# Second-layer products evicted one bank at a time, plain activations first: attention and a two-layer network in one Trainium2 kernel

## Chip, cores and metric

The kernel runs on one core of a Trainium2 chip. The metric is the device time of one execution in microseconds; smaller is better. Before the change the median of three runs is 333.38 us (333.01 to 333.63).

## What is computed

Attention over 8 batches of 8 heads, 576 queries each, with 16 extra "beacon" keys ahead of 576 causal ones and 64 numbers a head. Its output, 4608 tokens of 512 numbers, goes through two dense layers, 512 to 2048 to 512, with a leaky ReLU between:

```
scores = scale * np.matmul(q, k_all.transpose(0, 1, 3, 2))
scores = np.where(causal, -1000000000.0, scores)
a = softmax(scores)
x = (a @ v_all), heads side by side           # 4608 x 512
h = x @ w_in                                  # 4608 x 2048
g = np.maximum(0.01 * h, h)
out = g @ w_out                               # 4608 x 512, float32
```

## The kernel before

Two heads of one batch form a **group**; there are 32, numbered g, four to a batch. 512 tokens form a **chunk**; there are nine, numbered i. Attention of later groups and the two layers of earlier chunks are interleaved on TensorE in one order that the program writes out itself (`tc.manual_schedule`, L731): every engine runs its instructions in the order in which the Python issues them. The steps that matter here:

- **Score block** (`block`, L780): three stretches of 512 score columns for two heads (L314), exponentials on ScalarE (L329 and L333), triangles of the causal mask on GpSimd (L289). The first stretch takes two banks of the pool `ps_one`, the others the pool `ps_sc`.
- **Value step** `v(g, half)` (`value`, L374): 12 or 18 matmuls (L359) into a bank of `ps_one`, then reciprocal and multiplication on VectorE (L388, L389).
- **`x_turn(g)`** (L412): two DMA transposes on SyncE's queue (L417, L425) that put a group's output into `xT`, the first layer's input.
- **First-layer step** `u(i, fc)` (`up`, `moe1`, L431): four matmuls of 512 columns (L442) into a bank of `ps_one`; ScalarE's Prelu (L450) evicts them to `gT`. A chunk has 16. Chunk i can start when its last group's `x_turn` has landed: chunk 2 needs group 11, chunk 3 group 15, and so on.
- **Second-layer step** (`down`, `moe2`, L524): chunk 0 is multiplied plainly (L512). Chunks 1 to 8 use a scheme of Strassen and Winograd: `gT` is cut into four blocks a11, a12, a21, a22 by token half and by feature half, and seven products of sums replace eight. A product has two steps (tiles a and b, 128 tokens each) of eight matmuls of 256 columns (L539).

The left operands (`left`, L483) are plain blocks for products 1 (a11), 2 (a12) and 4 (a22); for 5, 6 and 3 they are the sums s1, s2, s4 in `gsum`, and for 7 the sum s3, which overwrites a21. VectorE makes the sums (`token_sums`, L469; L616), four adds for each half of the features; the second four can start only after the Prelu of the chunk's last first-layer step. They wait in the list `due`, and one is issued before each further step; before step 2 of a chunk the rest is issued at once (`add_all`, L638).

The products are built in the order 1, 6, 2, 7, 5, 4, 3 (`PRODUCTS`, L501). Product 2 is added on top of 1 in bank a, which is therefore open from 1 to 2; 4 on top of 7 in bank c; 3 on top of 5 in bank d. `combine` (L552) evicts: ScalarE copies 1, 2 and 5 (L565, L570, L576), VectorE adds the others (L567, L573, L577, L581, L585), and `store` (L591) writes quarter results to HBM by SyncE's queue. All of this, the first layer, the value steps and the score blocks' first stretches share the four banks of `ps_one`.

Which step comes next is decided by `fill` (L598): first and second layer in turn where both can go. The events of the groups (loads N from HBM by GpSimd, L171; key and query transposes T by SyncE, L179; blocks, value steps, `x_turn`) have due times, and the loop at L817 puts as many steps between them as their share of the work at hand. When a batch's last group is finished, three second-layer steps that were kept back (`KEPT`, L668) go first. Before a value step, the loop fills up to four steps since the last block, if no second-layer step is to be had (L826).

Of the kernel before, what the change touches and what calls it, by code (L numbers as in the profile page):

```python
# [8 lines left out]
FP32 = mybir.dt.float32  # L9
# [6 lines left out]
def kernel(  # L16
# [11 lines left out]
    nc = tc.nc  # L28
# [3 lines left out]
    DM = moe_w_in.shape[0]  # L32
# [6 lines left out]
    NCH = NTOK // 512  # L39
# [42 lines left out]
    opool = ctx.enter_context(tc.tile_pool(name="opool", bufs=2))  # L82
    ps_sc = ctx.enter_context(tc.tile_pool(name="ps_sc", bufs=2, space=bass.MemoryType.PSUM))
    ps_one = ctx.enter_context(tc.tile_pool(name="ps_one", bufs=4, space=bass.MemoryType.PSUM))
# [368 lines left out]
    ADD, SUB = ALU.add, ALU.subtract  # L453

    def weight_sums(part):
        b11, b12 = w_out_sb[:, 0:HF, 0:HD], w_out_sb[:, 0:HF, HD:DM]
        b21, b22 = w_out_sb[:, HF:NF, 0:HD], w_out_sb[:, HF:NF, HD:DM]
        t1, t2, t4 = (w_sum[:, i] for i in range(3))
        tt = nc.vector.tensor_tensor
        if part == 0:  # L460
            tt(out=t1, in0=b12, in1=b11, op=SUB)
            tt(out=t2, in0=b22, in1=t1, op=SUB)
            tt(out=t4, in0=b21, in1=t2, op=SUB)
        else:
            tt(out=b12, in0=b22, in1=b12, op=SUB)
# [17 lines left out]
    def left(i, n, fc, tile):  # L483
        t = slice(tile * 128, (tile + 1) * 128)
        if n == 1:
            return gT[i][:, fc, t]
        if n == 2:
            return gT[i][:, HF + fc, t]
        if n == 7:
            return gT[i][:, fc, HT + tile * 128 : HT + (tile + 1) * 128]  # L490
        if n == 4:
            return gT[i][:, HF + fc, HT + tile * 128 : HT + (tile + 1) * 128]
        return sums[i][{5: 0, 6: 1, 3: 2}[n]][:, fc, t]

    def right(n, fc):
        if n in (5, 6, 4):
            return w_sum[:, (5, 6, 4).index(n), fc]
        fc0, d0 = {1: (0, 0), 2: (HF, 0), 3: (HF, HD), 7: (0, HD)}[n]
        return w_out_sb[:, fc0 + fc, d0 : d0 + HD]

    PRODUCTS = (1, 6, 2, 7, 5, 4, 3)  # L501
    banks, parts = {}, {}

    def ND(i):
        return NF if i == 0 else 2 * len(PRODUCTS)

    def moe2_plain(i, t, quarter):
        if quarter == 0:
            banks["a"] = ps_one.tile([128, 512], FP32, name="acc", tag="one")
        acc = banks["a"]  # L510
        for fc in range(quarter * 4, quarter * 4 + 4):
            nc.tensor.matmul(  # L512
                out=acc,
                lhsT=gT[i][:, fc, t * 128 : (t + 1) * 128],
                rhs=w_out_sb[:, fc],
                start=(fc == 0),
                stop=(fc == NF - 1),
            )
        if quarter == 3:
            osb = opool.tile([128, DM], FP32, name="osb", bufs=3)  # L520
            nc.vector.tensor_copy(out=osb, in_=acc)
            nc.sync.dma_start(out=out[i * 512 + t * 128 : i * 512 + (t + 1) * 128], in_=osb)

    def moe2(i, n2):  # L524
        if i == 0:
            moe2_plain(i, n2 // 4, n2 % 4)
            if n2 == NF - 1:
                weight_sums(1)
            return
        n, tile = PRODUCTS[n2 // 2], n2 % 2  # L530
        bank = {1: "a", 2: "a", 6: "b", 7: "c", 4: "c", 5: "d", 3: "d"}[n]
        opens = n in (1, 6, 7, 5)
        apart = i == NCH - 1 and bank == "d"
        if opens and (tile == 0 or apart):
            banks[bank, tile] = ps_one.tile([128, 512], FP32, name="acc", tag="one")
        acc = banks[bank, tile if apart else 0]
        lo = 0 if apart else tile * HD
        for fc in range(HF):
            nc.tensor.matmul(  # L539
                out=acc[:, lo : lo + HD],  # L540
                lhsT=left(i, n, fc, tile),
                rhs=right(n, fc),
                start=(opens and lo == 0 and fc == 0),
                stop=(fc == HF - 1),
                skip_group_check=True,
            )
        if apart:
            combine(i, n, acc[:, 0:HD], (tile, tile + 1))
        elif tile == 1:
            combine(i, n, acc, (0, 2))  # L550

    def combine(i, n, acc, tiles):  # L552
        lo, hi = tiles[0] * HD, tiles[1] * HD

        def kept(name, bufs=1):
            if lo == 0 or name == "osb":
                parts[name] = opool.tile([128, 512], FP32, name=name, bufs=bufs)
            return parts[name][:, lo:hi]

        def part(name):  # L560
            return parts[name][:, lo:hi]

        tt = nc.vector.tensor_tensor
        if n == 1:
            nc.scalar.copy(out=kept("u2"), in_=acc)  # L565
        elif n == 6:
            tt(out=part("u2"), in0=acc, in1=part("u2"), op=ADD)  # L567
        elif n == 2:
            c = kept("osb", 3)
            nc.scalar.copy(out=c, in_=acc)  # L570
            store(i, 0, 0, tiles, c)
        elif n == 7:
            tt(out=kept("u3"), in0=acc, in1=part("u2"), op=ADD)  # L573
        elif n == 5:
            c = kept("p5")
            nc.scalar.copy(out=c, in_=acc)  # L576
            tt(out=part("u3"), in0=part("u3"), in1=c, op=ADD)  # L577
            store(i, 1, 1, tiles, part("u3"))
        elif n == 4:
            c = kept("osb", 3)  # L580
            tt(out=c, in0=acc, in1=part("u2"), op=ADD)  # L581
            store(i, 1, 0, tiles, c)
        elif n == 3:
            c = kept("osb", 3)
            tt(out=c, in0=acc, in1=part("u2"), op=ADD)  # L585
            store(i, 0, 1, tiles, c)

    def store(i, half, cols, tiles, c):
        t0 = i * 512 + half * HT + tiles[0] * 128
        n = tiles[1] - tiles[0]  # L590
        nc.sync.dma_start(  # L591
            out=out[t0 : t0 + n * 128, cols * HD : (cols + 1) * HD].rearrange("(t p) d -> p t d", p=128),
            in_=c.rearrange("p (t d) -> p t d", t=n),
        )

    done1, done2, at2, ready, turn, first_down, held = [0], [0], [0, 0], [0], [0], [0], [0]

    def fill():  # L598
        i1, fc = divmod(done1[0], NF)
        i2, n2 = at2  # L600
        can1 = i1 < ready[0] and (i1 < 2 or i2 > i1 - 2)
        can2 = i2 < NCH and i2 < i1 and done1[0] >= first_down[0]
        if held[0] and can2:
            held[0] -= 1
            down()
        elif can1 and (turn[0] == 0 or not can2):
            up()
        elif can2:
            down()
        return can1 or can2  # L610
# [8 lines left out]
    def add_all(i):  # L619
        while due and due[0][0] == i:  # L620
            add_due()
# [3 lines left out]
    def up():  # L625
        i1, n = divmod(done1[0], NF)
        assert i1 < ready[0]
        fc = n if i1 == 0 else n // 2 + n % 2 * HF
        moe1(i1, fc)
        add_due()  # L630
        done1[0] += 1
        turn[0] = 1
        if i1 and n % (2 * SLICE) == 2 * SLICE - 1:
            due.extend((i1, op) for op in token_sums(i1, n // 2 + 1 - SLICE, n // 2 + 1))

    def down():
        add_due()
        if at2[1] == 2:  # L638
            add_all(at2[0])
        moe2(*at2)  # L640
        done2[0] += 1
        at2[1] += 1
        if at2[1] == ND(at2[0]):
            at2[:] = at2[0] + 1, 0
        turn[0] = 0
# [19 lines left out]
            )  # L665

    NG = B * NPAIR
    KEPT = 3  # L668

    def has(g):  # L670
        return 0 <= g < NG
# [6 lines left out]
    def finish(g, eng=0):  # L678
        if eng < 2 and g in xs:
            x_transposes(g, (dve, act)[eng])  # L680
        ready[0] = chunks_with(g)
        if g % NPAIR == NPAIR - 1:
            turn[0] = 1
            held[0] = KEPT

    def run(steps):
        for step in steps.split():
# [52 lines left out]
    with order:  # L740
# [46 lines left out]
        def has_down():  # L787
            return at2[0] < done1[0] // NF

        since = 0  # L790
# [26 lines left out]
        for at, _, what, args in events:  # L817
            while w + 2 < len(ends) and at > ends[w + 1]:
                w, d0 = w + 1, done1[0] + done2[0]
            todo = NF * ready[0] + sum(ND(i) for i in range(ready[0])) - KEPT - d0  # L820
            aim = d0 + todo * (at - ends[w]) / (ends[w + 1] - ends[w])
            while done1[0] + done2[0] < aim and fill():
                pass
            if what is block:
                since = done1[0] + done2[0]
            elif what is value and not has_down():  # L826
                while done1[0] + done2[0] < since + 4 and fill():
                    pass
            what(*args)
        while at2[0] < NCH:  # L830
# [31 lines left out]
```

## Time and profile before

| | before |
|---|---|
| median of three runs | 333.38 us |
| profiled execution | 332.48 us |
| its span | 330.8 us |
| TensorE busy | 317.8 us (96%), 3401 matmuls recorded |
| ScalarE busy | 199.8 us (60%) |
| GpSimd busy | 183.2 us (55%), all of it in the first 276 us |
| VectorE busy | 132.5 us (40%) |
| first-layer matmuls L442 | 134.0 us, 615 recorded |
| second-layer matmuls L539 | 47.2 + 32.9 + 15.5 + 15.4 us, 896 recorded |

A time in the profile counts from the start of the span. PE is TensorE's matmul queue, PEld its weight loads, DVE VectorE, ACT ScalarE, POOL GpSimd, SP SyncE. A wait "A <- B" means that A's engine was idle until B ended. Some matmul records are missing, so counts are a little low.

### The profile page before, as it was taken

The numbers are of one execution on the slowest core, as the hardware profiler recorded it, in microseconds if no ns is written. First come the engines' busy times: TensorE is split into PE (matmuls) and PEld (weight loads), VectorE is DVE, ScalarE is ACT, GpSimd is POOL, SyncE is SP. The second block draws the span as 40 slices with busy tenths as digits, with TensorE's granted clock in tenths as the row PEclk, the third lists the DMA queues.
The fourth block names the chain that finished last, engine by engine and source line by source line (L and its number), as shares of the span: only waits on it lengthen the run. The fifth ranks groups of instructions, "written<-read, shape, count | busy, mean of one in ns | idle before, by whom it ended". The sixth has DMA issues, their size and how long they took to land.

```text
span 330.8 us, 8482 instructions
## 1 busy us (share of the span) xinstructions
PE 317.8 (96%) x3401; PEld 213.1 (64%) x3429; DVE 132.5 (40%) x280; ACT 199.8 (60%) x336; POOL 183.2 (55%) x354
## 2 busy tenths in 40 slices
PE   8999999999899999999999999998999999999996
PEld 5574555455586557844778888655875695466685
DVE  3572357126443145414621453334442642333343
ACT  4969861678665784578645865587458514644420
POOL 8895968979987884669546976686221000000000
PEclk9999999999999999999999999999999999999999
DMA  8999999999999999999989999999431113000113
GB/s 134 140 204 178 153 209 121 179 181 131 180 111 169 158 157 142 131 164 102 145 122 154 109 146 113 184 120 155 55 100 37 36 21 127 2 0 34 64 43 117
DMA packets 155929, 39.93 MB, mean 121 GB/s; under 512 B 143041, under 2 KB 153153, under 8 KB 155889
## 3 DMA queue, kind: packets, MB, share of 16 engines
q0 software_dynamic: 99824, 18.54, 83.1%
q1 hardware_dynamic: 55792, 20.77, 38.7%
q8 instruction: 27, 0.44, 0.6%
q14 instruction: 14, 0.11, 0.1%
q10 hardware_dynamic: 272, 0.07, 0.1%
HBM read 37.22 MB, written 9.44 MB: 141 GB/s over the span
## 4 chain that ended last, share of the span: by engine, by line
PE 76%; DMA 8%; ACT 5%; DVE 4%; POOL 4%; issue 2%; SPq 0%; ACTq 0%; POOLq 0%
PE acc L442 34%; PE acc L539 25%; PE av L359 7%; PE sc L314 5%; DMA w_out_sb<-in_moe_w_out_dram 4%; PE acc L512 4%; DMA v_aug<-in_v_dram 3%; DVE gsum L616 2%; ACT aT L333 2%; ACT aT L329 2%; ACT gT L450 1%; DVE x_nat L389 1%; POOL gsum L158 1%; DMA xT<-x_nat 1%; POOL v_aug L214 1%
## 5 line engine op out<-in xcount | busy, mean ns | idle before, releaser
L442 PE MATMUL acc<-xT,w_in_sb 128*128 128x512 bf16 (+1 forms) x615 | 134.0, 357 | 1.9 <-DMA xT<-x_nat 0.5
L450 ACT ACTIVATE gT<-acc 128x512 bf16<-128x512 f32 x144 | 83.0, 620 | 56.9 <-PE acc L442 55.4
L442 PEld LDWEIGHTS <-w_in_sb 128*128 128x128 bf16 x640 | 59.6, 98 | 53.6 <-issue 4.3
L289 POOL TENSOR_SCALAR_AFFINE_SELECT aT<-aT 128x256 bf16<-128x256 bf16 (+2 forms) x160 | 59.8, 403 | 60.9 <-ACT aT L329 38.7
L539 PEld LDWEIGHTS <-gT 128*128 128x128 bf16 x512 | 48.9, 98 | 11.2 <-ACT gT L450 2.3
L333 ACT ACTIVATE aT<-sc 128x1024 bf16<-128x1024 f32 (+3 forms) x64 | 51.7, 890 | 0.0
L539 PE MATMUL acc<-w_out_sb,gT 128*128 128x256 bf16 x384 | 47.2, 273 | 1.4 <-ACT gT L450 1.3
L329 ACT ACTIVATE aT<-sc 128x512 bf16<-128x512 f32 (+3 forms) x64 | 28.9, 520 | 25.3 <-PE sc L314 25.3
L359 PEld LDWEIGHTS <-aT 128*128 128x128 bf16 (+1 forms) x960 | 36.6, 98 | 9.3 <-issue 3.0
L539 PEld LDWEIGHTS <-gsum 128*128 128x128 bf16 x384 | 36.1, 98 | 8.8 <-DVE gsum L616 3.3
L359 PE MATMUL av<-v_aug,aT 128*128 128x65 bf16 (+1 forms) x960 | 39.5, 194 | 1.9 <-ACT aT L329 1.6
L214 POOL DMA_DIRECT2D v_aug<-in_v_dram x40 | 34.3, 866 | 4.3 <-DMA w_in_sb<-in_moe_w_in_dram 4.0
L171 POOL DMA_DIRECT2D q_nat<-in_q_dram x48 | 34.9, 734 | 0.7
L171 POOL DMA_DIRECT2D k_nat<-in_k_dram x48 | 34.8, 732 | 0.7 <-DMA w_out_sb<-in_moe_w_out_dram 0.4
L539 PE MATMUL acc<-w_sum,gsum 128*128 128x256 bf16 x256 | 32.9, 273 | 1.8 <-DVE gsum L616 1.7
L616 DVE TENSOR_TENSOR gsum<-gT 128x1024 bf16<-128x1024 bf16 x16 | 11.2, 697 | 53.9 <-ACT gT L450 53.9
L389 DVE TENSOR_TENSOR x_nat<-av,rec 128x384 bf16<-128x384 f32 (+1 forms) x64 | 31.4, 490 | 2.2
L388 DVE RECIPROCAL rec<-av 128x6 f32<-128x6 f32 (+1 forms) x64 | 11.9, 185 | 50.7 <-PE av L359 50.5
L276 ACT ACTIVATE aT<-sc 128x1024 bf16<-128x1024 f32 (+3 forms) x32 | 26.0, 874 | 3.7 <-PE sc L267 1.9
L314 PE MATMUL sc<-qT,kT 64*128 64x80 bf16 (+22 forms) x384 | 22.4, 250 | 1.2 <-PE acc L442 0.5
L314 PEld LDWEIGHTS <-kT 64*128 64x128 bf16 x384 | 13.3, 94 | 11.9 <-issue 8.9
L573 DVE TENSOR_TENSOR u<-acc,u 128x512 f32<-128x512 f32 x8 | 5.5, 691 | 27.2 <-PE acc L539 27.2
(63 smaller groups left out, 221.5 us busy)
## 6 DMA issues: line engine op xcount, KB each, us to landing
out_dram<-osb SPq DMA_DIRECT2D x27, 256.0 KB, 2.8
q_nat<-in_q_dram POOLq DMA_DIRECT2D x48, 72.0 KB, 4.8
k_nat<-in_k_dram POOLq DMA_DIRECT2D x48, 72.0 KB, 5.2
v_aug<-in_v_dram POOLq DMA_DIRECT2D x24, 128.0 KB, 6.4
w_in_sb<-in_moe_w_in_dram POOLq DMA_DIRECT2D x2, 1024.0 KB, 12.3
w_out_sb<-in_moe_w_out_dram POOLq DMA_DIRECT2D x2, 1024.0 KB, 11.6
out_dram<-u SPq DMA_DIRECT2D x7, 256.0 KB, 2.3
gsum<-in_q_dram POOLq DMA_DIRECT2D x8, 144.0 KB, 6.4
```

Of the source, the lines that this page charges most:

```text
L171: nc.gpsimd.dma_start(out=t[:, :, par], in_=(q, k)[which][b, 2 * hp + par].rearrange("(t p) d -> p t d", p=NR),)
L214: nc.gpsimd.dma_start(out=dst[lo : ROWS[c], c, :, 0:D], in_=v[b, :, OFF[c] : OFF[c] + n].rearrange("h p d -> p h d"),)
L276: nc.scalar.activation(out=aT[:, :, c0 : c0 + w], in_=sc[:, :, 0:w], func=AF.Exp, scale=0.125)
L289: nc.gpsimd.affine_select(out=view, in_=view, compare_op=ALU.is_ge, fill=0.0, base=128 - n if lo == 0 else 0, channel_multiplier=-1, patte ...
L314: nc.tensor.matmul(out=(sc[par] if apart else sc[:, par])[:, at : at + b - a], lhsT=kT[ps_, c * 128 : (c + 1) * 128], rhs=qT[ps_, q0 : q0 ...
L329: nc.scalar.activation(out=probs[g][:, par, lo:hi], in_=sc[par][:, at : at + hi - lo], func=AF.Exp, scale=0.125)
L333: nc.scalar.activation(out=probs[g][:, :, lo:hi], in_=sc[:, :, at : at + hi - lo], func=AF.Exp, scale=0.125)
L359: nc.tensor.matmul(out=avv[:, n, 0 : D + 1], lhsT=aT[0 : ROWS[c], par, a0 : a0 + 128], rhs=va[0 : ROWS[c], c, 2 * hp + par, :], start=(c = ...
L389: nc.vector.tensor_tensor(out=x_nat[:, t0:t1].rearrange("p t e d -> p (t e) d"), in0=avv[:, :, 0:D], in1=rec[:, n0:n1, None].to_broadcast( ...
L442: nc.tensor.matmul(out=acc[:, lo:hi], lhsT=w_in_cols(fc, j), rhs=xT[:, j, x0 : x0 + hi - lo], start=(j == 0), stop=(j == NJ - 1), skip_gro ...
L450: nc.scalar.activation(out=gT[i][:, fc, :], in_=acc, func=AF.Prelu, alpha=0.01)
L539: nc.tensor.matmul(out=acc[:, lo : lo + HD], lhsT=left(i, n, fc, tile), rhs=right(n, fc), start=(opens and lo == 0 and fc == 0), stop=(fc ...
```

## The change

Each product is now evicted as soon as its two steps are done, and opens and closes a bank of its own. The order is 1, 4, 6, 2, 7, 5, 3. ScalarE copies 1, 4 and 5 to SBUF tiles p1, p4, p5; VectorE makes the four results from these and from PSUM with two more adds a chunk, both on SBUF alone (in the last chunk one of the two is made in halves). The output tiles `osb`, three deep, are gone: p1, p4, u3 and p5, one deep, are stored instead, chunk 0's results too. The sums' remainder is issued before step 4. Of a chunk, four second-layer steps are counted out of the share of the work (`KEPT`), and two (`LEAD`) go first at a batch's end. When at most two second-layer steps of the chunk before are left (`LAST`), the first layer goes on and leaves them. Before a value step the loop now fills two steps if second-layer steps are to be had, and then takes these.

```
-    PRODUCTS = (1, 6, 2, 7, 5, 4, 3)
+    PRODUCTS = (1, 4, 6, 2, 7, 5, 3)
...
-            osb = opool.tile([128, DM], FP32, name="osb", bufs=3)
+            osb = opool.tile([128, DM], FP32, name=("p1", "p4", "p5", "u3")[t], bufs=1)
...
-        bank = {1: "a", 2: "a", 6: "b", 7: "c", 4: "c", 5: "d", 3: "d"}[n]
-        opens = n in (1, 6, 7, 5)
-        apart = i == NCH - 1 and bank == "d"
-        if opens and (tile == 0 or apart):
-            banks[bank, tile] = ps_one.tile([128, 512], FP32, name="acc", tag="one")
-        acc = banks[bank, tile if apart else 0]
+        apart = i == NCH - 1 and n2 >= 10
+        if tile == 0 or apart:
+            banks["p"] = ps_one.tile([128, 512], FP32, name="acc", tag="one")
+        acc = banks["p"]
...
-                start=(opens and lo == 0 and fc == 0),
+                start=(lo == 0 and fc == 0),
...
+        if n in (1, 4, 5):
+            nc.scalar.copy(out=part(f"p{n}", True), in_=acc)
+        if n == 6:
+            add(part("u2", True), acc, part("p1"))
         elif n == 2:
+            add(part("p1"), acc, part("p1"))
+            store(i, 0, 0, tiles, part("p1"))
         elif n == 7:
+            add(part("u3", True), acc, part("u2"))
+            add(part("p4"), part("u3"), part("p4"))
+            store(i, 1, 0, tiles, part("p4"))
         elif n == 5:
+            add(part("u3"), part("u3"), part("p5"))
             store(i, 1, 1, tiles, part("u3"))
+            add(part("p5"), part("u2"), part("p5"))
         elif n == 3:
+            add(part("p5"), acc, part("p5"))
+            store(i, 0, 1, tiles, part("p5"))
...
-        elif can1 and (turn[0] == 0 or not can2):
+        elif can1 and not (rest and can2) and (turn[0] == 0 or not can2 or (i1 == i2 + 1 and ND(i2) - n2 <= LAST)):
             up()
...
-        if at2[1] == 2:
+        if at2[1] == 4:
             add_all(at2[0])
...
-    KEPT = 3
+    KEPT, LEAD = 4, 2
...
-            held[0] = KEPT
+            held[0] = LEAD
...
-            elif what is value and not has_down():
-                while done1[0] + done2[0] < since + 4 and fill():
+            elif what is value:
+                while done1[0] + done2[0] < since + (2 if has_down() else 4) and fill(True):
                     pass
```

More of the change, by code (lines that the diff above doesn't have):

```diff
@@ L553, in combine, with part, add @@
         lo, hi = tiles[0] * HD, tiles[1] * HD
-        def kept(name, bufs=1):
-            if lo == 0 or name == "osb":
-                parts[name] = opool.tile([128, 512], FP32, name=name, bufs=bufs)
+        def part(name, new=False):
+            if new and lo == 0:
+                parts[name] = opool.tile([128, 512], FP32, name=name, bufs=1)
             return parts[name][:, lo:hi]
[L560 to L567, printed above, removed]
+        def add(to, x, y):
+            nc.vector.tensor_tensor(out=to, in0=x, in1=y, op=ADD)
+        if n in (1, 4, 5):
+            nc.scalar.copy(out=part(f"p{n}", True), in_=acc)
+        if n == 6:
+            add(part("u2", True), acc, part("p1"))
         elif n == 2:
-            c = kept("osb", 3)
-            nc.scalar.copy(out=c, in_=acc)
-            store(i, 0, 0, tiles, c)
+            add(part("p1"), acc, part("p1"))
+            store(i, 0, 0, tiles, part("p1"))
         elif n == 7:
-            tt(out=kept("u3"), in0=acc, in1=part("u2"), op=ADD)
+            add(part("u3", True), acc, part("u2"))
+            add(part("p4"), part("u3"), part("p4"))
+            store(i, 1, 0, tiles, part("p4"))
         elif n == 5:
-            c = kept("p5")
-            nc.scalar.copy(out=c, in_=acc)
-            tt(out=part("u3"), in0=part("u3"), in1=c, op=ADD)
+            add(part("u3"), part("u3"), part("p5"))
             store(i, 1, 1, tiles, part("u3"))
[L579 to L582, printed above, removed]
+            add(part("p5"), part("u2"), part("p5"))
         elif n == 3:
-            c = kept("osb", 3)
-            tt(out=c, in0=acc, in1=part("u2"), op=ADD)
-            store(i, 0, 1, tiles, c)
+            add(part("p5"), acc, part("p5"))
+            store(i, 0, 1, tiles, part("p5"))
     def store(i, half, cols, tiles, c):
@@ L596, with fill @@
     done1, done2, at2, ready, turn, first_down, held = [0], [0], [0, 0], [0], [0], [0], [0]
-    def fill():
+    LAST = 2
+    def fill(rest=False):
         i1, fc = divmod(done1[0], NF)
```

## The prediction, on record before the change was run

> **What bounds the kernel now.** I read the page's first part, then the waits, the timelines of the engines that the waits name, and last the chain. TensorE first:
>
> ```profile
> PE 317.8 (96%) x3401; PEld 213.1 (64%) x3429; DVE 132.5 (40%) x280; ACT 199.8 (60%) x336; POOL 183.2 (55%) x354
> ```
>
> It is busy 96% of 330.8 us and the change leaves it every matmul, so only its stalls can go. The waits (total, times, longest) say which:
>
> ```profile
> PEld L539 <- DVE gsum L616: 3.3, 6, 0.8
> ...
> PEld L539 <- ACT gT L450: 2.3, 3, 0.9
> ...
> PE acc L539 <- DVE gsum L616: 1.7, 5, 0.6
> PE av L359 <- ACT aT L329: 1.6, 3, 0.8
> ...
> PE acc L539 <- ACT gT L450: 1.3, 2, 0.7
> ...
> PE acc L442 <- DMA xT<-x_nat: 0.5, 1, 0.5
> ```
>
> The weight loads wait beside the matmuls behind them, so I count only the PE rows. On TensorE's timeline (start, length, then idle time and releaser in brackets) one chunk's turn from first to second layer is:
>
> ```profile
> 229.29 0.28 PE L539 MATMUL acc<-w_out_sb,gT 128*128 128x256 bf16 x1 [0.67 <-ACT gT L450]
> ...
> 230.65 0.60 PE L539 MATMUL acc<-w_sum,gsum 128*128 128x256 bf16 x4
> 231.80 0.61 PE L539 MATMUL acc<-w_sum,gsum 128*128 128x256 bf16 x4 [0.55 <-DVE gsum L616]
> ...
> 232.81 1.04 PE L539 MATMUL acc<-w_sum,gsum 128*128 128x256 bf16 x8
> 233.68 0.49 PE L539 MATMUL acc<-w_out_sb,gT 128*128 128x256 bf16 x3
> ```
>
> Product 1 waits for the Prelu of the last but one first-layer step; product 6 waits, halfway, for VectorE's sums. A third kind, in another window, is a value step that wants a PSUM bank while two banks are held by half-built products:
>
> ```profile
> 169.45 0.83 PE L314 MATMUL sc<-qT,kT 64*128 64x176 bf16 x14
> 171.08 0.53 PE L359 MATMUL av<-v_aug,aT 128*128 128x65 bf16 x12 [0.80 <-ACT aT L329]
> ```
>
> A group's record runs some 0.16 us past its last issue slot (the eight matmuls at 232.81 are 1.04 long, yet the next group starts 0.87 later), so a gap of g costs g + 0.16. I use 0.87 for a step of either layer.
>
> The second limit is the feed. The chain shows TensorE waiting for an activation transpose on SyncE's queue:
>
> ```profile
> 101.80 0.56 SPq L417
> ...
> 102.42 3.73 DMA xT<-x_nat
> 106.19 0.59 PE acc L442 x2
> ```
>
> That is the first step u(2,0) of chunk 2, waiting for x_turn(11). On SyncE, in order, that transpose stood behind the key transpose of group 15, and this behind its loads from GpSimd:
>
> ```profile
> 99.25 1.20 SPq L179 DMA_TRANSPOSE kT<-k_nat  x1
> 100.54 1.83 SPq L417 DMA_TRANSPOSE xT<-x_nat  x1
> 102.42 1.22 SPq L425 DMA_TRANSPOSE xT<-x_nat  x1
> ```
>
> GpSimd's timeline shows what set those loads:
>
> ```profile
> 78.49 1.86 POOL L289 TENSOR_SCALAR_AFFINE_SELECT aT<-aT 128x256 bf16<-128x256 bf16 x3 [0.44 <-ACT aT L329]
> 80.60 0.41 POOL L289 TENSOR_SCALAR_AFFINE_SELECT aT<-aT 128x256 bf16<-128x256 bf16 x1 [0.25 <-ACT aT L333]
> ...
> 91.69 1.45 POOL L171 DMA_DIRECT2D k_nat<-in_k_dram  x2
> ```
>
> From 81 to 98 us GpSimd shows no idle time: its loads there do not come earlier because TensorE is faster.
>
> [...] here L567 (from PSUM) and L577 (SBUF alone) both take 692 ns, which I use. [...] at 101.00 VectorE ends a 3.19 us wait for ScalarE's copy of product 5, and only then does the reciprocal behind it run.
>
> **The change, part by part.** The base is the profiled execution: 332.48 us, 1.7 of it outside the span; the runs' median, 333.38, is 0.9 above it.
>
> *Waits removed.* In the new order products 1 and 4 come first, so between the last Prelu and product 6 stand four steps (3.5 us) in place of two, often with two products of the chunk before ahead of them. The sums need two adds of 0.69 after that Prelu: product 6 came at most 0.55 late, so 1.74 more covers it. Product 1's waits (0.63 at 87.13, 0.67 at 229.29) are covered where two old steps or both value steps (0.9) now stand before it. The value waits go because no bank is held across products: each turns over after two steps. Gaps up to 121.5 us: 0.19 (71.06, a first-layer step wanting a bank), 0.63, 0.28 (90.47, the same for a score tile), 0.30; 1.40 and four times 0.16 = 2.04. Later: 0.55, 0.17, 0.53, 0.80, 0.27, 0.67, 0.55, 0.17 = 3.71, eight times 0.16 = 1.28, and 0.31 inside the group at 123.49 (1.35 long, not 1.04): 5.30. Together 7.3.
>
> *What is late next.* u(2,0). The new order has chunk 1's product 3 (two steps) and a score block (0.78) after it, not before: 2 x 0.87 + 0.78 = 2.52 of work moves behind. TensorE, which would have been there at 106.19 - 0.69 = 105.50, arrives at 105.50 - 2.52 - 2.04 = 100.94. The feed hardly moves: the score block before GpSimd's solid stretch comes some 1.2 earlier (a step of 0.87, and the wait at 71.06), but GpSimd was idle only 0.44 then, so x_turn(11) lands at 106.15 - 0.44 = 105.71. TensorE waits 4.8 us: the first 2.04 are lost again, and from there 2.52 - 0.44 = **2.08 more** remains. Before that, group 14's key transpose (in use 1.3 us after landing) is overtaken too; that wait lies inside the same one. The later chunks' first steps stood 5 to 8 us behind their transposes and move 0 to 2.5: no wait. The wait for group 17's keys at 121.48 (0.36 + 0.16 = **0.52**) goes, as TensorE is then later.
>
> *Waits added.* Product 3 is opened, then held over up to nine first-layer steps, so three times a step just after a score block needs the bank of the step just before it: 0.66 us of matmuls against 0.20 (last slot 176.38 to Prelu 176.58) + 0.60 (Prelu) + 0.05: 0.19 each, 0.57. If ScalarE is 0.6 behind, 0.8 each: 2.4; below nothing is excluded, since a wait can't give time. What queues behind is all of TensorE, and through it the next block's exponentials. The block behind u(2,0) comes 2.5 late, so group 18's loads do too; its 3.5 us of cover shrink to under 1: 0 to 1, I take 0.3. Sum **0.87**.
>
> *Work added.* 17 adds of 0.69 or 0.43 on VectorE, 11 us on an engine 40% busy. Those for products 7 and 5 lie ahead of reciprocals; the tightest bank behind them has 1.4 us of matmuls against 0.69 more in the queue: nothing; with that cover gone, 0.69 a chunk. ScalarE keeps three copies a chunk (0.60, now for 1, 4, 5), SyncE four stores, GpSimd all it had. Product 7's store waits for two adds, not one: 0.7 on SyncE, hidden while SyncE is behind its producers. The single buffers p1 to p5 are rewritten 10 us or more after their store: nothing. The tail is as before, 5b's two adds of 0.43 ending before 3b's matmuls: 0 to 0.1.
>
> **Sum**: -5.30 - 0.52 + 2.08 + 0.87 = -2.87. Span 327.9, execution 329.6, on the median's scale 333.38 - 2.87 = **330.5**.
>
> **Rivals.** *The feed gives more.* If x_turn(11) lands 2 us sooner (TensorE's own steps no longer delay group 14's block, and the transposes find a shorter queue), 328.5. For it: those transposes took 3.7 to 7.4 us, so there is room. Against: SyncE waited for the key loads, which GpSimd paces. *The removed waits turn into others*: Prelu late by 0.8 three times (2.4 for 0.57) and group 18 by 1.0 (for 0.3): 330.5 + 2.5 = 333.0, no change. For it: two banks serve the first layer there. Against: ScalarE idles 0.28 before each Prelu of such a stretch, so it isn't behind. *Slower*: x_turn(11) meets a full queue, as x_turn(10) did (issued 92.20, its SyncE row 3.15 long, some 7.3 to landing where x_turn(11) took 3.7), because GpSimd's loads for group 17 now start earlier beside it. Each us there is a us at the end; from a landing at 108.6 the gain is gone, at 109.6 the time is 330.5 + 3.9 = 334.4. Against: the loads move by 1.3 at most.
>
> **Numbers.** Forecast 0.60 (330.5, own spread 329.5 to 331.8), more gain 0.20 (328.5), no change 0.12, slower 0.08. A measurement tells 0.2% (0.7 us) from none: faster 0.79, same 0.13 (a bit of the forecast's upper edge included), slower 0.08. The range runs from 328.5 to 333.2: the upper end takes in the 2.4 for the Prelus, the lower the 2 us of feed.
>
> **Signs.** Right: no PE wait on the sums (gsum, line L610 after the change), none of av on aT; one long PE wait on xT near 101 to 106 us, 4 to 5 us; VectorE some 11 us busier. If that wait is under 2 us, the feed was paced by TensorE and the gain is larger. If first-layer steps wait for Prelus by more than 1 us in all, the held bank is dearer than I say. Wrong altogether: x_turn(11) landing after 108.6.

## The result and the profile after

| | before | after |
|---|---|---|
| median of 20 runs each, in turn on one chip | 332.84 us (331.38 to 338.48) | 333.74 us (332.06 to 337.40) |
| ratio, 95% interval | | 1.0038 (1.0016 to 1.0060) |
| profiled execution, its span | 332.48, 330.8 us | 333.21, 331.5 us |
| mean granted TensorE clock, profiled execution | 0.999 | 0.995 |

The kernel became slower by 0.9 us where 2.87 less was forecast. On the scale of these 20 runs the forecast is 332.84 - 2.87 = 329.97, so 3.8 us are missing. Here and below, medians are of all runs, while ratios, and averages of runs with a like clock, leave out the few executions that fell into a slower state of the chip.

The page's first part, after:

```profile
PE 319.8 (96%) x3429; PEld 213.5 (64%) x3429; DVE 145.9 (44%) x297; ACT 200.1 (60%) x336; POOL 187.5 (57%) x354
```

VectorE is 13.4 us busier (11 were forecast) and GpSimd, which got no new work, 4.3. The waits of TensorE (total, times, longest):

```profile
PE sc L314 <- POOL kT L229: 2.7, 1, 2.7
...
PE av L359 <- DVE x_nat L389: 0.5, 2, 0.3
PE acc L442 <- DMA xT<-x_nat: 0.5, 1, 0.5
...
PE acc L442 <- ACT gT L450: 0.4, 2, 0.2
```

No product waits for the sums any more, none for a Prelu, and no value step for ScalarE's exponentials. In the chunk whose turn was shown before, TensorE's timeline now has no idle time:

```profile
230.19 1.91 PE L537 MATMUL acc<-w_out_sb,gT 128*128 128x256 bf16 x16
...
232.59 1.91 PE L537 MATMUL acc<-w_sum,gT 128*128 128x256 bf16 x16
```

These are products 1 and 4; product 6, at 235.21, follows a score block without idle time too. What was meant to go has gone, then. What came instead stands at the start of chunk 2, on the same timeline:

```profile
96.41 0.52 PE L314 MATMUL sc<-qT,kT 64*128 64x144 bf16 x10
99.59 0.50 PE L314 MATMUL sc<-qT,kT 64*128 64x256 bf16 x6 [2.66 <-POOL kT L229]
100.02 3.57 PE L537 MATMUL acc<-w_out_sb,gT 128*128 128x256 bf16 x16
...
108.32 0.38 PE L442 MATMUL acc<-xT,w_in_sb 128*128 128x512 bf16 x1 [0.53 <-DMA xT<-x_nat]
```

Three losses lie here. A score block waits 2.66 us for group 14's keys; the last of them to arrive is the key transpose, landed at 99.45, not the column copy that the row names: TensorE starts 0.14 after it, the same as in run 7 below (99.49 and 99.63). Then 16 second-layer matmuls take 3.57, not the 1.91 of the chunk above, 1.66 too long. Then u(2,0) waits 0.53 for x_turn(11), which lands at 108.28 by the chain:

```profile
103.66 4.62 DMA xT<-x_nat
```

The windows of this stretch (length, busy time of TensorE, its loads, VectorE, ScalarE and GpSimd, then the granted clock; the last two columns are the DMA's) say what the second loss is:

```profile
90.00:100.00 10.00, 7.34 (x105) 5.77 (x103) 4.32 (x8) 5.04 (x10) 10.00 (x19) 1.00 1.95 129
100.00:110.00 10.00, 9.47 (x96) 6.82 (x94) 4.78 (x9) 3.85 (x7) 5.61 (x12) 0.83 1.50 162
```

The granted clock was 0.83 over 10 us. In narrower windows it was 0.50 from 100.1 to 103.3 us, and 1.00 before 99.9 and after 103.5: 1.7 us lost in some 3.4 at half the clock. GpSimd was busy for the whole ten microseconds before. It was late for two reasons. At 75.62 it was 1.93 behind before already (73.69 there), as this execution as a whole was. And where it could have caught up, its selects (L289) took longer:

```profile
79.98 3.36 POOL L289 TENSOR_SCALAR_AFFINE_SELECT aT<-aT 128x256 bf16<-128x256 bf16 x4
...
88.96 3.57 POOL L289 TENSOR_SCALAR_AFFINE_SELECT aT<-aT 128x256 bf16<-128x256 bf16 x5
```

That is 0.84 and 0.71 each. Before, three took 1.86 and one 0.41 at 78.5 to 81.0, and then five took 2.66, also with some of VectorE's adds beside them:

```profile
86.78 2.66 POOL L289 TENSOR_SCALAR_AFFINE_SELECT aT<-aT 128x256 bf16<-128x256 bf16 x5
```

So group 15's key loads were issued at 94.79, 3.10 later than before. VectorE worked beside the first four on SBUF alone:

```profile
79.97 1.51 DVE L465 TENSOR_TENSOR w_out_sb<-w_out_sb 128x2048 bf16<-128x2048 bf16 x1
81.42 0.88 DVE L610 TENSOR_TENSOR gT<-gT 128x1024 bf16<-128x1024 bf16 x1
```

Both sides took longer side by side: the first four selects 0.84 each here and 0.34 to 0.41 in a kernel where none of VectorE's adds ran beside them, L465 1.51 here and 1.22 in that kernel (experiment 7). What they hold each other up with, the traces don't show.

### The profile page after: what moved, and what is told of

Read it like the earlier page. It is cut to its first block, busy times and chain, and to the rows that moved or that the text cites. A ratio compares the mean times of both kernels' runs of the same rounds, so it can differ in the third digit from the quotient of the medians.

```text
span 331.5 us, 8537 instructions
## 1 busy us (share of the span) xinstructions
PE 319.8 (96%) x3429; PEld 213.5 (64%) x3429; DVE 145.9 (44%) x297; ACT 200.1 (60%) x336; POOL 187.5 (57%) x354
## 3 DMA queue, kind: packets, MB, share of 16 engines
q1 hardware_dynamic: 55792, 20.77, 36.8%
## 4 chain that ended last, share of the span: by engine, by line
PE 67%; DMA 16%; ACT 4%; POOL 4%; DVE 4%; issue 3%; SPq 1%; DVEq 0%; ACTq 0%; POOLq 0%
PE acc L442 28%; PE acc L537 25%; PE av L359 6%; PE sc L314 5%; DMA gsum<-in_q_dram 5%; DMA xT<-x_nat 3%; DMA w_out_sb<-in_moe_w_out_dram 3%; DMA v_aug<-in_v_dram 3%; ACT aT L333 3%; PE acc L512 2%; DMA k_nat<-in_k_dram 2%; POOL aT L289 1%; DVE p L559 1%; DVE u L559 1%; POOL gsum L158 1%
## 5 line engine op out<-in xcount | busy, mean ns | idle before, releaser
L442 PE MATMUL acc<-xT,w_in_sb 128*128 128x512 bf16 (+1 forms) x640 | 136.8, 358 | 1.4 <-DMA xT<-x_nat 0.5
L289 POOL TENSOR_SCALAR_AFFINE_SELECT aT<-aT 128x256 bf16<-128x256 bf16 (+2 forms) x160 | 64.0, 429 | 55.3 <-ACT aT L329 34.1
L537 PE MATMUL acc<-w_out_sb,gT 128*128 128x256 bf16 x384 | 47.9, 279 | 0.0
L562 ACT COPY p<-acc 128x512 f32<-128x512 f32 (+1 forms) x25 | 14.5, 581 | 41.2 <-PE acc L537 37.6
L537 PE MATMUL acc<-w_sum,gsum 128*128 128x256 bf16 x256 | 31.9, 273 | 0.0
```

The costliest lines, as they stand in the source:

```text
L289: nc.gpsimd.affine_select(out=view, in_=view, compare_op=ALU.is_ge, fill=0.0, base=128 - n if lo == 0 else 0, channel_multiplier=-1, patte ...
L442: nc.tensor.matmul(out=acc[:, lo:hi], lhsT=w_in_cols(fc, j), rhs=xT[:, j, x0 : x0 + hi - lo], start=(j == 0), stop=(j == NJ - 1), skip_gro ...
L537: nc.tensor.matmul(out=acc[:, lo : lo + HD], lhsT=left(i, n, fc, tile), rhs=right(n, fc), start=(lo == 0 and fc == 0), stop=(fc == HF - 1) ...
```

## The experiments

**The theory**: the new products gain about what was forecast, and the changed order of steps (KEPT, LEAD, LAST and the fill before value steps) gives it back at one place, where chunk 2's start and group 14's block now come before their feed. **Rivals**: the halved clock alone takes the gain; the held product 3 and the new fill cost a little in every chunk; the new products themselves cost.

| run | kernel | median, us | ratio to before, 95% |
|---|---|---|---|
| 1 | after, TensorE kept busy before group 14's block | 333.81 | 1.0024 (1.0000 to 1.0048) |
| 2 | new products, old order of steps | 328.08 | 0.9872 (0.9841 to 0.9903) |
| 3 | old products, changed order | 336.08 | 1.0111 (1.0073 to 1.0149) |
| 4 | before, with four rests of TensorE | one execution, 351.09 | |
| 5 | after, KEPT 3 and LEAD 3 | 327.28 | 0.9823 (0.9782 to 0.9865) |
| 6 | run 2, plain products not first | 330.01 | 0.9901 (0.9859 to 0.9943) |
| 7 | after, VectorE's adds apart from the selects | 331.47 | 0.9944 (0.9919 to 0.9969) |
| 8 | new products, changed order from chunk 2 on | 328.85 | 0.9847 (0.9803 to 0.9892) |
| 9 | after, KEPT 3 alone | 334.73 | 1.0044 (1.0022 to 1.0066) |
| 10 | after, LEAD 3 alone | 331.60 | 0.9957 (0.9931 to 0.9983) |
| 11 | run 5 up to chunk 2's start, after from there | 329.11 | 0.9886 (0.9829 to 0.9943) |

**1. Is it the clock?** Ten blank matmuls of 512 columns stand ahead of the stretch that first needs group 14.

```
+        for _ in range(warm):
+            nc.tensor.matmul(
+                out=sc[:, 0, 0:512].rearrange("p (r w) -> p r w", w=128),
+                lhsT=blank,
+                rhs=blank[:, None, 0:128].to_broadcast([128, 4, 128]),
...
-                stretch(parts, apart=n == 0)
+                stretch(parts, apart=n == 0, warm=10 if any(g == 14 and lo == 0 for g, lo, _ in parts) else 0)
```

> The changed kernel with ten matmuls of 512 columns on zeros (2.2 us of TensorE work) put where TensorE idled 2.66 us for group 14's keys; nothing else differs, and the results are the same. Theory C (the loss is the clock: after that idle time the matmuls were issued at half pace for 3.4 us): the idle time shrinks to some 0.5 us, the slow pace after it is gone, and the kernel is 1.7 us or more faster than the changed one: ratio to before 0.996 or less. Rival W (the loss is in the added adds and evictions, wherever they lie): the clock makes no difference, ratio about 1.004 as for the changed kernel.

Measured: 333.81 us, no gain, so the ratio of at most 0.996 that one theory gave was missed. The idle time at group 14's block is gone and the matmuls after it have their full pace (16 in 1.92), but TensorE's timeline then reads:

```profile
107.89 0.58 PE L451 MATMUL acc<-xT,w_in_sb 128*128 128x512 bf16 x1 [3.27 <-DMA xT<-x_nat]
108.41 1.46 PE L323 MATMUL sc<-qT,kT 64*128 64x272 bf16 x16
```

(This kernel's lines stand nine further down.) TensorE arrives earlier at u(2,0), waits 3.27 us for x_turn(11), landed at 107.85, and slows down after that (16 score matmuls in 1.46, not 0.83). Although TensorE was ready earlier, u(2,0) began when its transpose landed: the feed sets it, and the clock is a second loss on top. The 22 runs say how large: the six with a mean clock of 1.000 took 331.65 us on average, the thirteen at 0.995 334.15, and before 332.68 at 1.000. So without a slow stretch this kernel gains 1.0 us, not 2.87: the clock is part of the loss, not all of it.

**2 and 3. The products or the order?** Run 2 is the kernel after with the order's rules of before, run 3 the kernel before with the changed rules:

```
-    KEPT, LEAD = 4, 2
+    KEPT, LEAD = 3, 3
...
-        elif can1 and not (rest and can2) and (turn[0] == 0 or not can2 or (i1 == i2 + 1 and ND(i2) - n2 <= LAST)):
+        elif can1 and (turn[0] == 0 or not can2):
...
-            elif what is value:
-                while done1[0] + done2[0] < since + (2 if has_down() else 4) and fill(True):
+            elif what is value and not has_down():
+                while done1[0] + done2[0] < since + 4 and fill():
```

> The changed kernel with the order of steps of before (three steps kept, three to lead, first layer and second in turn, no filling ahead of value steps while second-layer steps are to be had): new products, banks and evictions alone. Theory C: group 14's block keeps its place, so it waits for its keys by 0.7 to 1.5 us[...]; u(2,0) keeps its place too; the waits for sums and banks after 122 us go: some 3 to 4 us faster than before, ratio 0.988 to 0.992. Rival W: the new products bring nothing or a loss, ratio 1.000 to 1.004.

> The kernel before with the changed order of steps alone (four kept, two to lead, LAST, filling ahead of value steps), products and banks as before. Theory C: group 14's block and u(2,0) come early against their feed, and the waits for sums and banks stay: a wait of 1 to 2.5 us on group 14's keys, ratio 1.002 to 1.010. Rival W: as the products are those of before, ratio 0.995 to 1.000.

Measured: 328.08 us for the products alone, 336.08 for the order alone. The products gain 4.8 us against the 332.83 of before, measured in turn with them; the order costs 3.3 without them and 5.7 with them. Run 3 shows the loss at the same place, 4.18 us of waiting for group 14's keys at 100.20 (1 to 2.5 expected), and is a little slower than the range said; a bank is held over there too, and TensorE waits six times more, 0.36 to 0.59 each. In run 2 group 14's block, expected to wait 0.7 to 1.5, doesn't wait; u(2,0) still waits 1.27 us and product 1 three times for a Prelu (0.63, 0.67, 0.67).

**4. What idle time halves the clock?** The kernel before, with four rests of TensorE in chunk 8's first layer: a blank matmul, a Prelu, some selects on GpSimd, then a matmul that needs them.

```
+    RESTS = {0: 2, 5: 4, 10: 5, 15: 7}
...
+        if i1 == NCH - 1 and n in RESTS:
+            rest(RESTS[n])
```

> The kernel before with four rests put into TensorE's work late in the kernel, where nothing is fed any more, at steps 0, 5, 10 and 15 of the last chunk's first layer, some 9 us apart: a matmul on zeros, a Prelu of it, then 2, 4, 5 and 7 triangle selects on GpSimd in a chain, then a matmul that needs them: idle times of some 1.5, 2.3, 2.7 and 3.5 us. Theory C: after the last one or two the next matmuls are issued at half pace for some 3 us, after the first not. Rival W: the pace after all four is the full one, and the slow pace in the changed kernel had another cause.

Measured, on TensorE's timeline (the row that ends each of the first three rests, and work after the first and third):

```profile
292.84 0.23 PE L636 MATMUL av<-blank,aT 128*128 128x128 bf16 x1 [2.23 <-POOL aT L289]
...
295.19 1.91 PE L442 MATMUL acc<-xT,w_in_sb 128*128 128x512 bf16 x4
...
306.34 0.23 PE L636 MATMUL av<-blank,aT 128*128 128x128 bf16 x1 [2.80 <-POOL aT L289]
...
318.27 0.29 PE L636 MATMUL av<-blank,aT 128*128 128x128 bf16 x1 [2.91 <-POOL aT L289]
318.35 1.91 PE L442 MATMUL acc<-xT,w_in_sb 128*128 128x512 bf16 x4
```

Four first-layer matmuls normally take 1.03. After 2.23 us of rest they were slow from 0.9 us on, after 2.80 not at all, after 2.91 at once, after 4.18 within the first four (1.59); a slow stretch cost 1.5 to 1.7 us. The rests came out longer than planned, and the first, which was to have no effect, had one. Length alone does not decide between 2.2 and 2.9 us, and 2.66 was enough in after; what else decides was not shown. The granted clock of this execution was 0.75 from 295 to 300 us, 1.00 from 300 to 315, 0.80 and 0.86 in the two windows of 5 us from 315 on, and 0.66 from 330 to 335. The pace fell by half: in after the 16 matmuls at 100.02 took 212 ns from one to the next (3.39 to the group behind them), the 16 at 230.19 took 109 (1.75). At half pace a stretch is twice as long as what it costs, by which those here were 3.0 to 3.4 us long, an estimate; in after it was 3.4.

**5. Two numbers back.** `KEPT, LEAD = 3, 3` in the kernel after, nothing else. u(2,0) then comes after product 3 and the block of groups 14 and 15, as before the change.

> The kernel after, with the two numbers of before (KEPT and LEAD 3 and 3, not 4 and 2); LAST and the fill before value steps stay as changed. The first layer's step u(2,0) then comes after product 3 and the score block, as before the change, and the steps ahead of group 14's block are one less. Theory A (what costs is the place of chunk 2's start and of group 14's block against their feed): 327.5 to 329, as in the kernel with the whole old order, one wait of 1 to 1.5 us for x_turn(11), no half pace. Theory B (the held product 3 and the new fill before value steps cost in every chunk): 330.5 or more, with small waits of first-layer steps in chunks 3 to 8.

Measured: 327.28 us, ratio 0.9823. That is 0.2 under theory A's range, and 6.5 us less than after, for two numbers. TensorE at chunk 2's start:

```profile
100.61 1.91 PE L537 MATMUL acc<-w_out_sb,gsum 128*128 128x256 bf16 x16
102.45 0.83 PE L314 MATMUL sc<-qT,kT 64*128 64x272 bf16 x16
...
105.04 2.97 PE L442 MATMUL acc<-xT,w_in_sb 128*128 128x512 bf16 x12 [1.00 <-DMA xT<-x_nat]
```

Product 3 and the block of groups 14 and 15 now run while x_turn(11) is under way, one wait of 1.00 us is left, and the clock stays full (1.00 in each window from 60 to 110 us). LAST and the new fill are still in this kernel, so by themselves they cost nothing that the runs can tell.

**6. Banks or plain products first?** In run 2, the order 1, 6, 4, 2, 7, 5, 3 and the sums' remainder before step 2.

```
-    PRODUCTS = (1, 4, 6, 2, 7, 5, 3)
+    PRODUCTS = (1, 6, 4, 2, 7, 5, 3)
...
-        if at2[1] == 4:
+        if at2[1] == 2:
```

> The kernel with the new products and the old order of steps (328.08 us), but product 6 second and product 4 third, the sums' remainder issued before step 2: each product still has its own bank and goes out at once, but the products on plain activations no longer lead. If the gain of the new products comes from both parts: TensorE waits again for the sums, some 2 to 2.5 us in all, and the time is 330 to 330.8; the waits of value steps for a bank stay away. If the banks alone bring it: 328 to 328.6. If the bank turnover brings nothing: 332 or more.

Measured: 330.01 us, within the first range. The waits for the sums are back:

```profile
PE acc L537 <- DVE gsum L610: 1.5, 5, 0.6
```

With 0.16 for each of the five gaps they cost 2.3 us, and no value step waits for a bank. So both parts bring something; the intervals of runs 2 and 6 overlap, so their shares are read from the waits alone.

**7. Do VectorE's adds make GpSimd late?** The order of TensorE's steps is that of after. The last weight sum and two of chunk 1's sums are issued some 5 us later, behind a value step.

```
-            if n2 == NF - 1:
-                weight_sums(1)
...
+    def away():
+        return 25 <= done1[0] < 28 and done2[0] == 16
...
-        while due and n:
+        while due and n and not away():
...
+        if done1[0] == 28:
+            weight_sums(1)
```

> The kernel after, its order of steps as it is; only VectorE's last weight sum (L465) and two of chunk 1's sums (L610) are issued some 5 us later, so that GpSimd's four selects at 80 us no longer run beside them. If their meeting is what made GpSimd late: those selects take 0.4 to 0.6 each, not 0.84, the key loads of groups 14 and 15 come 0.9 to 1.4 earlier, the wait of 2.66 for group 14's keys shrinks to 1.2 to 1.8, x_turn(11) lands 1 to 1.5 earlier, and the time is 331 to 332.5. If GpSimd is only late because its blocks come later: selects and landing within 0.4 of what they were, 333 to 334.

Measured: 331.47 us, 2.3 less than after. GpSimd's selects, and TensorE's two waits:

```profile
80.89 1.02 POOL L289 TENSOR_SCALAR_AFFINE_SELECT aT<-aT 128x256 bf16<-128x256 bf16 x3
82.24 0.41 POOL L289 TENSOR_SCALAR_AFFINE_SELECT aT<-aT 128x256 bf16<-128x256 bf16 x1 [0.34 <-ACT aT L333]
...
88.40 1.74 POOL L289 TENSOR_SCALAR_AFFINE_SELECT aT<-aT 128x256 bf16<-128x256 bf16 x5
```

```profile
99.63 0.50 PE L314 MATMUL sc<-qT,kT 64*128 64x256 bf16 x6 [1.84 <-DMA kT<-k_nat]
100.07 1.92 PE L535 MATMUL acc<-w_out_sb,gT 128*128 128x256 bf16 x16
...
106.67 0.38 PE L442 MATMUL acc<-xT,w_in_sb 128*128 128x512 bf16 x1 [0.48 <-DMA xT<-x_nat]
```

The chain has the two landings, of group 14's keys (99.49) and of x_turn(11) (106.63):

```profile
92.48 7.01 DMA kT<-k_nat
...
102.53 4.10 DMA xT<-x_nat
```

The selects take 0.34 to 0.41 each, group 15's key loads are issued at 92.62, 2.17 earlier than in after, and x_turn(11) lands 1.65 earlier, although this execution reached group 8's block 0.71 later (62.59 against 61.88). Counted from that block, it landed after 44.0 us here, after 46.4 in after and after 47.0 in run 1, which has the adds beside the selects too. Group 14's keys are another matter: they landed no earlier than in after (99.45), and counted from group 8's block after 36.9 us here, 37.6 in after and 36.8 in run 1. Their wait is shorter because TensorE came 0.86 later, so the adds are not shown to delay them.

The matmuls after the 1.84 us of idle time keep their pace. Not every run did: of this kernel's 20 comparable runs 12 had a mean clock of 1.000 and took 330.38 us on average, five had 0.995 and took 332.01, and two had 0.993 and 0.994. Runs with one slow stretch were thus 1.6 us longer at the end as well (2.5 in run 1); part of that may be the longer wait that led to it.

**8 to 11. Which part of the order, and where?** Run 8 has the old rules until chunk 1's second layer is done and the changed ones from there; 9 and 10 put one of the two numbers back alone (`KEPT, LEAD = 3, 2` and `4, 3`); 11 is run 5 until that point and after from there.

```
+    def late():
+        return at2[0] >= 2
...
-            held[0] = LEAD
+            held[0] = LEAD if late() else 3
...
-            todo = NF * ready[0] + sum(ND(i) for i in range(ready[0])) - KEPT - d0
+            todo = NF * ready[0] + sum(ND(i) for i in range(ready[0])) - (KEPT if late() else 3) - d0
```

(These two edits are in 8 and 11; run 8 puts LAST and the fill under the same condition.)

> The new products, with the old order of steps up to the end of chunk 1's second layer and the changed order (KEPT, LEAD, LAST, fill before value steps) from there on. Theory A (the changed order costs at the start of chunk 2 alone): 327 to 328.3, as fast as with the old order throughout or up to 1 us faster, since the two waits of product 1 for a Prelu in chunks 3 and 6 (0.67 each) may go and some of 0.2 come. Theory B (it costs in every chunk): 330.5 or more.

> The kernel after with KEPT = 3 alone (LEAD stays 2). By the order of its steps the last weight sum on VectorE still comes after the block of group 10, beside GpSimd's selects, and chunk 2's step u(2,0) still stands ahead of group 14's block; one second-layer step more stands before it. If both of these are the cause, most of the loss stays: selects at 80 us near 0.8 each, a wait of 1.5 to 2.5 us for group 14's keys or for x_turn(11), 330.5 to 332.5. If KEPT alone was the fault: 327 to 328.5.

> The kernel after with LEAD = 3 alone (KEPT stays 4). By the order of its steps the last weight sum comes before the block of group 10, clear of the selects, and u(2,0) stands behind group 14's block, with one second-layer step less before it than in the kernel with 3 and 3 (327.28 us). If the place of these two is the cause: selects at 80 us at 0.4 to 0.6 each, a wait of 1.5 to 2.5 us at u(2,0) or at group 14's keys, and 327.5 to 330. If KEPT = 4 is the fault by itself: 332 or more.

> The new products with KEPT and LEAD at 3 and 3 up to the end of chunk 1's second layer, and the changed order after it. If the feed of chunk 2's start is the only thing that the changed order spoils, this is the fastest or level with the fastest: 326.3 to 327.6; the two waits of product 1 for a Prelu in chunks 3 and 6 (0.67 each, and 0.16 a gap) are gone and waits of 0.2 to 0.3 stand in their place. If the changed order costs something later too: 328.5 or more.

Measured: run 8, 328.85 us: the changed order from chunk 2 on costs nothing that the runs can tell, so the loss sits before it, as in theory A (0.5 above its range, 327 to 328.3). Run 11, 329.11, is 1.5 above the range that called it the fastest, where its text said that something later costs too. Its trace doesn't show that: after u(2,0) TensorE waits 1.05 us there and 1.34 in run 5. The intervals of runs 2, 5, 8 and 11 overlap, and which of them is fastest stays open. Runs 5 and 11 have the same steps up to u(2,0), yet x_turn(11) landed at 105.00 and 106.93: the executions differ by 1.8 us when they reach group 8's block (59.84 and 61.68), after the first loads.

Run 10, 331.60, missed its range by 1.6: LEAD 3 alone takes the weight sum out of the selects' way (0.48 each), but u(2,0) stands one step nearer to x_turn(11) and waits 1.49, and the rest of chunks 2 to 8 shows seven waits for banks, Prelus and VectorE of 0.19 to 0.53, 2.45 in all. Run 9, 334.73, missed by 2.2: KEPT 3 alone leaves u(2,0) ahead of the block of groups 14 and 15. There TensorE waits 3.14 us for x_turn(11) (landed 107.82) and slows down:

```profile
79.57 1.02 POOL L289 TENSOR_SCALAR_AFFINE_SELECT aT<-aT 128x256 bf16<-128x256 bf16 x3
```

```profile
107.86 0.59 PE L442 MATMUL acc<-xT,w_in_sb 128*128 128x512 bf16 x1 [3.14 <-DMA xT<-x_nat]
108.38 1.46 PE L314 MATMUL sc<-qT,kT 64*128 64x272 bf16 x16
```

Three of the four selects at 80 us were short, against what was expected, and the gain is gone all the same: x_turn(11), landing 46.4 us after group 8's block as in after, can be late without them (its first transpose took 2.08 us on SyncE's queue, 1.22 in after and in run 7). Also, product 3, of which only one step is then held over, makes first-layer steps wait 0.53 twice and others 0.17 to 0.39. So neither number is the fault alone; the place of the two steps is.

## Why the prediction was wrong, point by point

- **Waits removed, 7.3 us**: right. All are gone from the trace, and run 2, which has only the products, gains 4.8 us while u(2,0) takes 1.27 of it and product 1 keeps three waits.
- **What is late next**: this step failed, in its size and in two assumptions. The mechanism was right: 2.52 us of work stand behind u(2,0), and TensorE loses 2.66 + 1.66 + 0.53 = 4.85 us ahead of it, where 4.8 were forecast; that these agree is luck, since TensorE and the landing both came some 2.5 later than forecast. But x_turn(11) was to land at 105.71 and landed at 108.28, 2.57 later, so the net loss was 108.32 - 106.19 + 2.52 = 4.65 us instead of 2.08. "The feed hardly moves" was wrong. The order moved VectorE's weight sum and two of the sums of chunk 1 one block later, onto GpSimd's selects; with these apart the landing came 1.65 us earlier and the median 2.3 (run 7; part of the 2.3 is the slow stretch, which most runs there don't have). I had counted VectorE's work as hidden without asking what its adds do to the selects beside them (0.84 each, not 0.34 to 0.41), and had read GpSimd's solid stretch from 81 to 98 us as DMA issues that nothing changes: 4.4 us of it are selects. The rest of the 2.57, 0.92, goes with a late start: this execution reached group 8's block 1.85 later than before (61.88 against 60.03), of which 0.44 is u(1,0), now ahead of a second-layer step and waiting for VectorE. How much of the remainder is chance of one execution, the runs don't say; run 1, with the same steps up to here, was there at 60.82.
- **That wait is one wait for xT**: wrong. Group 14's keys came first and took most of it; I had put them inside the same wait at no price. That was right for the profiled sum, where the halved clock lies before u(2,0) and is covered by the late landing (without it TensorE would have waited 0.53 + 1.66 there). It was not right over the runs: every run of after had a mean clock of 0.995 or less, and a mean of 0.995 over 331.5 us is 1.66 us, one slow stretch. Those at 0.995 took 333.0 on average, those at 0.988 and 0.990, which by that sum is two, 334.4 and 335.4. I had no price for an idle TensorE beyond the idle time.
- **Waits added, 0.87**: mechanism right, 0.7 too small. The held bank made first-layer steps wait 0.22 twice (0.19 three times forecast), and group 18's keys made nothing wait. Two value steps waited 0.27 and 0.26 for VectorE, whose queue had the new add in front of the reciprocal:

```profile
245.78 0.84 DVE L559 TENSOR_TENSOR u<-u,p 128x512 f32<-128x512 f32 x1 [3.27 <-ACT p L562]
246.65 0.69 DVE L559 TENSOR_TENSOR p<-u,p 128x512 f32<-128x512 f32 x1
247.26 0.18 DVE L388 RECIPROCAL rec<-av 128x4 f32<-128x4 f32 x1
```

  At 247.95 TensorE's next value step got its bank, after 0.26. With 0.16 a gap, the four waits after u(2,0) cost 2 x 0.38 + 2 x 0.42 = 1.6. From u(2,0) to the end after was 2.52 + (330.78 - 106.19) - (331.50 - 108.32) = 3.93 us better where 4.95 were forecast; 0.7 of the difference is these waits, 0.3 I could not place.
- **Work added**: right in its amount (13.4 us on VectorE, some of it adds made longer by the selects), wrong in being free: see the two points above.
- **The sum**: 2.57 in the feed and 1.0 later make up the 0.73 + 2.87 = 3.6 us by which the profiled execution missed.
- **Rivals**: the slower one said that each microsecond of late landing is one at the end, and gave 334.4; that held. Its cause did not: x_turn(11) was issued at 103.66 and took 4.62, with a SyncE row of 1.22, where x_turn(10)'s in before was 3.15; the transposes ahead of it were late because GpSimd's loads were. The one where the feed gives more is excluded.
- **Signs**: no wait for the sums and a busier VectorE came true and told nothing of the time; the sign "landing after 108.6" was missed by 0.3, with the gain gone all the same.

## What to carry to other kernels

A gain from removed waits lasts only up to the next thing that is fed from elsewhere: before changing an order of steps, list what each moved step needs, when it lands, and which engine makes it, and move work in front of the late one, not behind. Count every engine that the order moves, also those with time to spare: a few adds on an engine 40% busy made another engine's loads late (issued at 94.79 in after, at 92.62 with the adds apart). And test a change that bundles arithmetic with a new order as two: here the first gave 1.3% and the second took it back.

## What the runs showed of the hardware that was not expected

- GpSimd's select of 256 columns took 0.34 to 0.41 us where none of VectorE's adds ran beside it (run 7) and 0.71 to 0.84 beside adds of two SBUF operands (after), and VectorE's add of 2048 columns 1.51 (after) instead of 1.22 (run 7).
- TensorE's matmuls slowed down to about half their pace after idle times of 2.23 and 2.91 (run 4), 2.66 (after), 3.14 (run 9), 3.27 (run 1) and 4.18 us (runs 3 and 4), and not after 1.84 (in the profiled execution of run 7) and 2.80 (run 4). In after the granted clock was then 0.50 for some 3.4 us. A slow stretch cost 1.5 to 1.7 us where it lay (run 4 and after).
- Two kernels with the same steps up to there (runs 5 and 11) differed by 1.8 us after the first loads, at 60 us (59.84 and 61.68), in their profiled executions.
